# W2 in a ring of row tiles, the second half's products first, and an early turn of the inverse table, in a gated mix of a long convolution and a token MLP

## The chip, the cores and the metric

The kernel runs on one core of a Trainium2 chip. Its engines work side by side, each through its own list of instructions: TensorE (PE) multiplies matrices, VectorE (DVE) and ScalarE (ACT) work on tensors, GpSimd (POOL) here mostly issues the DMAs that add to their target, and SyncE (SP) issues all other DMAs. The metric is device microseconds of one execution.

## The reference

The inputs are q, k, v and x = q of [2048, 640], a long filter per channel, and two weight matrices. The output is `g * a + (1 - g) * b`:

- g is a sigmoid of the row sum of `x * gate_w`, one number per row.
- a = q * (y + kv * ssm_D), where kv = shift(k) * v with four taps per channel, and y is the causal convolution of kv with the filter along the 2048 rows. The reference takes it by FFT of length 4096.
- b is a token MLP: layernorm of x, then `gelu(h^T W1 + b1) W2 + b2`, with W1 [2048, 1536] and W2 [1536, 2048] mixing the rows.

```python
y_f = kv_f * kf_f[None, :, :, :]
y = irfft2(y_f, (1, L))[:, 0, :S, :] + kv * ssm_D
u = gelu(einsum("bsd,sf->bdf", layernorm(x), w1) + b1)
b = einsum("bdf,fs->bds", u, w2) + b2      # transposed back
return g * (q * y) + (1 - g) * b
```

## The kernel before

**The convolution** is a transform written as matmuls. The rows are split by residues, the forward transforms of the filter (W) and of kv (A) are matmuls with a table FTB of sines, and VectorE mixes residues by adds and subtracts (`mixing`, `mixing_acc`). The spectra lie in slots of 2560 columns in the big tiles C[0] to C[3] and SS. V0, V1 are those of the filter and A0, A1 those of kv; each has two groups, 0 and 1, and each group two slots. A slot holds a real part (component 0) and an imaginary one (component 1), so a step on both slots of a group and both parts is 5120 columns wide and a step on one part is 2560.

The two halves of the output need the products `A0 * V0` and `A1 + ...` of complex numbers. Before the products `cross(g)` (L1165) multiplies A0 into V1, in four steps per slot with one DMA that adds a term; V1 then holds a term that is added to A1's product. `product` (L1130) multiplies a group in place: in full it is two multiplies of 5120 columns (into the scratch tiles T0, T1), a subtract and an add. With `late` it is one multiply of 5120 and three steps of 2560, and the second cross term goes by a DMA that adds it to the result. `acc_dma` (L1146) adds V1[g] to A1[g] with two such DMAs. The order is cross 0, cross 1, A0[0], A0[1] (both late), A1[0], A1[1] (both in full, each followed by its `acc_dma`). Then `invmix` (L1177) mixes the two groups of a half in eight steps, and `inverse` (L1196) runs 64 matmuls per half with the table, ScalarE scales by the gate, and VectorE multiplies by q. The first half is Z0 from A0, the second Z1 from A1. Matmuls of `inverse` read the table after it was put in another order: four DMA transposes turn FTB into GTB, and four ScalarE copies ("gil", L1082) write GTB back over FTB. They may run once the forward transforms are done. Before, they come after the inner matmuls, the copies tied to an output tile of the MLP.

**The MLP**: the inner product (m1) is 12 tiles `ft` of 32 matmuls, W1 being the stationary side and X the moving one, W1 coming in three column groups through two buffers `ring[0]` and `ring[1]` of 16 tiles [128, 512] each (`ring[(ft // 4) % 2]`). A GELU on ScalarE makes tile ft of GT. The outer product (m2) is 16 tiles of 24 matmuls, four for each quarter hk of W2's columns. A quarter is [128, 12, 512], loaded in two DMAs of six row tiles. Quarters 0 and 2 lie over ring[1], quarters 1 and 3 over ring[0] (L600), so quarter 1 waits for the last inner tile and quarters 2 and 3 for the outer tiles two quarters before.

**The gate**: `x * gate_w` goes through three small buffers gq that lie on GTB (L589); ScalarE sums them. The inverse's output buffers cgb lie there too.

**The order** of every engine's list is worked out ahead, by a planner (`_Sched`). Each operation has a planned duration, and each engine takes, of the operations ready by the plan, the one with the lowest `prio`, which is its index where none is given. m1 and m2 have priorities above 10^6, so they fill PE wherever the convolution has nothing ready; at most two of the four PSUM slots may hold MLP tiles. An accumulating DMA is planned at 1.2 us to issue, its bytes at 365 GB/s and 8 us to land. `after` means only that the other operation has started in the plan; chain=True orders the SP loads that carry it in this way. On the chip the order of each list is fixed, and each instruction waits by semaphores for what it reads and overwrites.

Of the kernel before, what the change touches and what calls it, by code (L numbers as in the profile page):

```python
# [510 lines left out]
def _build(nc, A_q, A_k, A_v, A_shift_k, A_ssm_k, A_ssm_D, B_x, B_w1, B_b1, B_w2, B_b2, gate_w, out):  # L511
# [10 lines left out]
    with ExitStack() as es:  # L522
# [13 lines left out]
        def alloc(name, shape, dtype, at=None):  # L536
            size = mybir.dt.size(dtype)
            for s_ in shape[1:]:
                size *= s_
            if at is None:  # L540
                off = cur[0]
                cur[0] = (off + size + 63) // 64 * 64
            else:
                off = at
            assert off % 4 == 0 and off + size <= top, f"SBUF overflow {name}: {off}+{size} > {top}"
            h = nc.alloc_sbuf_tensor_at(name, list(shape), dtype, offset=off)
            T.reg_sbuf(h, off)
            return h

        def base_of(h):  # L550
            return T.mem[h.name][1]
# [34 lines left out]
        dif = alloc("dif", [128, 128], I32, at=base_of(SS) + 64 + 1024)  # L586
        dif2 = alloc("dif2", [128, 32], I32, at=base_of(SS) + 64 + 1536)
        KT = [alloc(f"KT{i}", [128, NG, KTW], BF16) for i in range(2)]
        gq = [alloc(f"gq{i}", [128, 2, D], BF16, at=base_of(GTB) + 2560 * i) for i in range(3)]  # L589
        ssm = alloc("ssm", [128, ND, S], BF16, at=base_of(C[3]))  # L590
        wT = alloc("wT", [128, 4, 4, D], BF16, at=base_of(C[2]))
        vkv0 = alloc("vkv0", [128, 2, 4, D], BF16, at=base_of(C[3]))
# [4 lines left out]
        kn = [alloc(f"kn{i}", [128, 4, D], BF16, at=base_of(ring[1]) + 5120 * i) for i in range(2)]  # L597
        kp = [alloc("kp0", [128, NG, 128], BF16, at=base_of(ring[1]) + 10240), alloc("kp1", [128, NG, 128], BF16, at=base_of(GTB))]
        pint = alloc("pint", [128, 4, 2, 2, 256], I32, at=base_of(ring[1]))
        W2 = [alloc(f"W2_{i}", [128, FT, 512], BF16, at=base_of(ring[(i + 1) % 2])) for i in range(2)]  # L600
        O1 = alloc("O1", [128, 4, 4, D], BF16, at=base_of(X))
        tm = [alloc(f"tm{i}", [128, 2, 4, D], BF16, at=E_base + 2 * SL * 2 * i) for i in range(2)]
        q_lo = alloc("q_lo", [128, 2, 4, D], BF16, at=base_of(C[1]) + 2 * SL * 2)
# [111 lines left out]
        def dr(t, off, ap):  # L715
            return bass.AP(tensor=t.tensor, offset=t.offset + off, ap=ap)
# [22 lines left out]
        def w1_load(c, hk):  # L739
            dma(ring[c % 2][:, 4 * hk:4 * hk + 4, :], dr(B_w1, 512 * hk * F + 512 * c, [[4 * F, 128], [F, 4], [1, 512]]), 128 * 4096, chain=True)  # L740
# [239 lines left out]
        for hk in range(4):  # L980
            w1_load(1, hk)

        def v1mix(Wh, Ws, Vh, Vs):
            for i in range(2):
                dma(V(Vh, (Vs + i) * SL, [[1280, 2], [1, 1280]]), V(Wh, (Ws + i) * SL + 1280, [[-1280, 2], [1, 1280]]),
                    128 * 5120, stream="POOL", prio=0, accum=True)
# [58 lines left out]
        for ft in range(FT):  # L1045
            if ft == 4:
                for hk in range(4):
                    w1_load(2, hk)
            vt = _VT("mlp")
            r = ring[(ft // 4) % 2]  # L1050
            col = 128 * (ft % 4)
            for hk in range(4):
                items = []
                for p in range(4):
                    for ci in range(2):
                        items.append((chk(ci), r[:, 4 * hk + p, col:col + 128], X[:, hk, p, 320 * ci:320 * ci + 320],
                                      hk == 0 and p == 0, hk == 3 and p == 3))
                mms(vt, items, prio=10 ** 6 + 4 * ft + hk, name="m1")
            g_ = act(GT[:, ft, :].rearrange("p (a b) -> p a b", a=2), two, ACT.Gelu_apprx_tanh, bias=cc[:, 16 + ft:17 + ft], vt=vt, prio=0, name="gelu")
            if ft == 0:  # L1060
                act(gq[2][:, 0, :], gwb[:, :], ACT.Copy, acc=gws[:, :], name="gws").after.add(g_)
            if ft in (1, 3, 5, 7):
                hk = ft // 2
                for a in range(2):
                    gb = gq[(2 * hk + a) % 3]
                    tt("DVE", gb[:, :, :], X[:, hk, 2 * a:2 * a + 2, :], V(gwb, 0, [[0, 2], [1, D]]), ALU.mult)
                    for b in range(2):
                        t = 4 * hk + 2 * a + b
                        act(gb[:, b, :], gb[:, b, :], ACT.Copy, acc=gacc[:, t:t + 1], name="gsum")
# [7 lines left out]
        tt("DVE", c2[:, :].rearrange("p (a b) -> p a b", a=4), omg[:, :].rearrange("p (a b) -> p a b", a=4), b2f, ALU.mult, mode=1, prio=0)  # L1077

        gils = []
        for p in range(4):  # L1080
            dma(GTB[:, p, :, :, :, :].rearrange("q a b c d -> q (a b c) d"), FTB[:, p, :, :, :, :].rearrange("q a b c d -> q (a b c) d"), 128 * 2048, rate=200.0, transpose=True, prio=10 ** 5)
            gil = act(V(FTB, 1024 * p, [[1, 2], [256, 4], [2, 128]]), V(GTB, 1024 * p, [[512, 2], [128, 4], [1, 128]]), ACT.Copy, prio=10 ** 5, name="gil")  # L1082
            gils.append(gil)

        HORD = (0, 1, 2, 3)
        lastvt = []
        for n_, hk in enumerate(HORD):
            W2h = W2[n_ % 2]
            for a in range(2):
                w2last = dma(W2h[:, 6 * a:6 * a + 6, :], dr(B_w2, a * 6 * 128 * S + 512 * hk, [[S, 128], [128 * S, 6], [1, 512]]), 128 * 6144)  # L1090
            for p in range(4):
                vt = _VT("mlp")
                t = 4 * hk + p
                last_ = n_ == 3 and p == 3
                order = [(ft, ci) for ci in range(2) for ft in range(FT)] if last_ else [(ft, ci) for ft in range(FT) for ci in range(2)]
                na = 2 if last_ else 3
                for a in range(na):
                    items = []
                    for ft, ci in order[a * (24 // na):(a + 1) * (24 // na)]:
                        items.append((chk(ci), V(W2h, ft * 512 + p, [[4, 128]]), GT[:, ft, 320 * ci:320 * ci + 320], ft == 0, ft == FT - 1))  # L1100
                    mms(vt, items, prio=2 * 10 ** 6 + 4 * (4 * n_ + p) + a, name="m2")
                    if last_:
                        vt.keep = True
                        lastvt.append(vt)
                if not last_:
                    o_ = act(O1[:, hk, p, :].rearrange("p (a b) -> p a b", a=2), two, ACT.Identity, bias=c2[:, t:t + 1], scale=omg[:, t:t + 1], vt=vt, name="o1")
                    if n_ == 1 and p == 2:
                        for g in gils:
                            g.after.add(o_)

        A0 = {0: (C[2], 2), 1: (C[1], 0)}
        A1 = {0: (C[3], 2), 1: (C[3], 0)}
# [14 lines left out]

        npr = [0]

        def product(dst, a, v, late=False):  # L1130
            tt("DVE", P2(T0), P2(a), P2(v), ALU.mult)
            if late:
                n_ = npr[0] % 2
                npr[0] += 1
                tt("DVE", V(q_hi, n_ * SL, [[1280, 2], [1, 1280]]), H(a, 1), H(v, 0), ALU.mult)
                tt("DVE", H(dst, 1), H(a, 0), H(v, 1), ALU.mult)
                tt("DVE", H(dst, 0), H(T0, 0), H(T0, 1), ALU.subtract)
                dma(H(dst, 1), V(q_hi, n_ * SL, [[1280, 2], [1, 1280]]), 128 * 5120, stream="POOL", prio=0, accum=True)
# [38 lines left out]
        def invmix(Ya, Yb, sc, z0, z2):  # L1177
            def sl(h, s):
                return V(h, s * SL, [[1, SL]])

            def pr(h, s, rev=False):
                return V(h, s * SL + (1280 if rev else 0), [[-1280 if rev else 1280, 2], [1, 1280]])
            (ha, sa), (hb, sb), (hs, ss) = Ya, Yb, sc
            tt("DVE", sl(hs, ss), sl(ha, sa), sl(ha, sa + 1), ALU.add)
            tt("DVE", sl(hs, ss + 1), sl(hb, sb), sl(hb, sb + 1), ALU.add)
            tt("DVE", sl(ha, sa), sl(ha, sa), sl(ha, sa + 1), ALU.subtract)
            tt("DVE", sl(hb, sb), sl(hb, sb), sl(hb, sb + 1), ALU.subtract)
            tt("DVE", sl(ha, sa + 1), sl(hs, ss), sl(hs, ss + 1), ALU.add)
# [54 lines left out]
        Z0 = invmix(A0[0], A0[1], C3a, None, None)  # L1243
# [40 lines left out]
```

## Time and profile before

| | |
|---|---|
| median of 4 runs | 188.74 us (187.06 to 191.86) |
| profiled execution | 191.69 us |
| its span | 189.6 us |
| PE busy | 179.2 us (94%), 1389 matmuls |
| VectorE busy | 169.6 us (89%) |
| ScalarE busy | 117.3 us (62%) |
| GpSimd busy | 49.9 us (26%) |
| granted clock of PE | 0.991 |
| DMA | 42.86 MB, 226 GB/s |

The span runs from the first to the last instruction of the profiled execution. A slice of the page is a fortieth of the span, 4.74 us. In the waits, the first number is the sum in us, then how often, then the longest. PE's 384 inner and 384 outer matmuls and the 352 of the transforms of 320 columns follow each other at 0.136 us (24 of an outer tile in 3.26 us), though a single one is shown with 299 ns, as they overlap.

### The profile page before, as it was taken

To read this page: it belongs to the slowest core of one execution; us is meant where nothing else is said; L and a number is where in the kernel's file an instruction comes from. 1 tells how busy PE (TensorE), PEld (TensorE's weight loads), DVE (VectorE), ACT (ScalarE), POOL (GpSimd) and SP (SyncE) were. 2 spreads that over 40 slices of the span, in tenths; PEclk is the share of its full clock that TensorE was granted. 3 is DMA by queue.
4 is the path that set the end of the run, shared out by engine and by line. 5 is a ranking of instruction groups with operands and counts; after the bars stand their busy time and mean duration, and the time that the engine had idled before them with its cause. 6 is when DMAs were issued, how large, how long until landed. Compare 5 with 4: busy or idle time off the path is not lost.

```text
span 189.6 us, 3344 instructions
## 1 busy us (share of the span) xinstructions
PE 179.2 (94%) x1389; PEld 130.1 (69%) x1390; DVE 169.6 (89%) x200; ACT 117.3 (62%) x176; POOL 49.9 (26%) x41
## 2 busy tenths in 40 slices
PE   7999899989999998999999999999999999939994
PEld 3565486658778675766777778868888866826683
DVE  8699895999699999999889999999999998498553
ACT  5599987799999999169972111312493157314730
POOL 4059604599000252002212110102050504320000
PEclk9999999999999999999999999999999999997999
DMA  5999999899992399994899999999989999994332
GB/s 158 381 409 371 388 213 240 340 420 212 165 348 60 111 165 193 266 238 91 140 207 274 112 134 124 177 298 322 288 230 262 251 263 299 201 232 107 138 107 104
DMA packets 38206, 42.86 MB, mean 226 GB/s; under 512 B 15787, under 2 KB 31280, under 8 KB 38192
## 3 DMA queue, kind: packets, MB, share of 16 engines
q1 hardware_dynamic: 33232, 32.16, 58.5%
q0 software_dynamic: 4928, 10.49, 33.6%
q8 instruction: 11, 0.18, 0.4%
q14 instruction: 3, 0.02, 0.0%
q10 hardware_dynamic: 32, 0.01, 0.0%
HBM read 25.87 MB, written 2.62 MB: 150 GB/s over the span
## 4 chain that ended last, share of the span: by engine, by line
PE 38%; DVE 26%; ACT 19%; DMA 11%; issue 4%; POOL 0%; SPq 0%; DVEq 0%
PE pp L293 38%; DVE C L624 14%; ACT C L668 10%; DMA C<-C 8%; DVE tm L624 7%; ACT gq L668 5%; DVE q_hi L624 3%; DMA ssm<-in_A_ssm_k_dram 3%; ACT GT L668 2%; ACT FTB L668 1%; DVE SS L624 1%; ACT L668 1%; ACT wT L668 1%; POOL C L262 0%; DVE O L680 0%
## 5 line engine op out<-in xcount | busy, mean ns | idle before, releaser
L293 PE MATMUL pp<-X,ring 128*128 128x320 bf16 x384 | 54.9, 299 | 0.7 <-ACT GT L668 0.7
L293 PE MATMUL pp<-GT,W 128*128 128x320 bf16 x384 | 53.0, 299 | 0.3 <-DMA W<-in_B_w_dram 0.3
L624 DVE TENSOR_TENSOR C<-C 128x2560 bf16<-128x2560 bf16 (+2 forms) x34 | 51.7, 1564 | 0.1
L293 PEld LDWEIGHTS pp<-GT,W 128*128 128x128 bf16 x384 | 43.3, 114 | 9.6 <-DMA W<-in_B_w_dram 0.9
L293 PEld LDWEIGHTS pp<-X,ring 128*128 128x128 bf16 x384 | 37.3, 98 | 15.3 <-issue 1.0
L668 ACT ACTIVATE C<-pp 128x640 bf16<-128x640 f32 x64 | 40.2, 722 | 4.2 <-PE pp L293 4.1
L668 ACT ACTIVATE O<-pp,c,omg 128x640 bf16<-128x640 f32 x15 | 13.2, 881 | 30.8 <-PE pp L293 30.8
L262 POOL DMA_DIRECT2D C<-C x8 | 9.9, 1359 | 49.9 <-DVE C L624 46.4
L293 PE MATMUL pp<-wT,FTB 128*128 128x320 bf16 x128 | 19.9, 301 | 2.0 <-ACT C L668 1.2
L668 ACT ACTIVATE GT<-pp,cc 128x640 bf16<-128x640 f32 x12 | 9.6, 799 | 15.4 <-PE pp L293 15.4
L668 ACT ACTIVATE cgb<-pp,gg 128x640 bf16<-128x640 f32 x16 | 12.7, 793 | 10.3 <-PE pp L293 10.3
L293 PEld LDWEIGHTS pp<-wT,FTB 128*128 128x128 bf16 x128 | 11.0, 98 | 10.1 <-ACT C L668 4.8
L293 PE MATMUL pp<-C,FTB 128*128 128x320 bf16 x96 | 15.0, 321 | 2.9 <-DVE C L624 2.9
L913 DVE BATCH_NORM_STATS2 stats<-X 128x6 f32<-128x320 bf16 x32 | 13.7, 464 | 1.7 <-DMA X<-in_A_q_dram 1.7
L293 PEld LDWEIGHTS pp<-C,FTB 128*128 128x128 bf16 x96 | 9.5, 105 | 8.2 <-issue 3.2
L262 POOL DMA_DIRECT2D C<-q_hi x6 | 5.9, 977 | 32.4 <-DVE C L624 28.8
L624 DVE TENSOR_TENSOR tm<-C,C 128x2560 bf16<-128x2560 bf16 (+1 forms) x7 | 14.3, 2058 | 0.0
L624 DVE TENSOR_TENSOR SS<-C 128x2560 bf16<-128x2560 bf16 x8 | 11.6, 1487 | 2.6 <-DMA C<-C 2.5
L1016 POOL COPY KT<-KT 128x20 bf16<-128x20 bf16 x1 | 12.4, 12379 | 3.1 <-DMA KT<-kp 3.1
L624 DVE TENSOR_TENSOR C<-tm 128x2560 bf16<-128x2560 bf16 (+1 forms) x10 | 12.0, 1221 | 0.1
L668 ACT ACTIVATE gq<-gq 128x640 bf16<-128x640 bf16 x16 | 11.8, 743 | 0.0
L668 ACT ACTIVATE wT<-pp 128x1024 bf16<-128x1024 f32 x10 | 9.6, 1032 | 1.6 <-PE pp L293 1.6
(72 smaller groups left out, 197.8 us busy)
## 6 DMA issues: line engine op xcount, KB each, us to landing
ring<-in_B_w_dram SPq DMA_DIRECT2D x12, 512.0 KB, 10.3
W<-in_B_w_dram SPq DMA_DIRECT2D x8, 768.0 KB, 9.6
C<-C POOLq DMA_DIRECT2D x8, 640.0 KB, 10.7
X<-in_A_q_dram SPq DMA_DIRECT2D x4, 640.0 KB, 9.0
kn<-in_A_k_dram SPq DMA_DIRECT2D x4, 640.0 KB, 8.4
out_dram<-O SPq DMA_DIRECT2D x7, 320.0 KB, 3.4
ssm<-in_A_ssm_k_dram SPq DMA_DIRECT2D x3, 512.0 KB, 6.4
vkv<-in_A_v_dram SPq DMA_DIRECT2D x2, 640.0 KB, 5.4
```

Of the source, the lines that this page charges most:

```text
L262: ins = engobj.dma_start(out_ap, in_ap, accum_op=ALU.add, max_dma_last_dim=2560)
L293: ins = self.nc.tensor.matmul(ps_ap, lhsT=lhsT, rhs=rhs, start=start, stop=stop, skip_group_check=True)
L624: o_ = SC.add(eng, d, lambda s: T.op(eng, lambda e: e.tensor_tensor(o, a, b, op), rd, [o]), rd, [o], prio=prio, name="tt")
L668: return T.op("ACT", lambda e: e.activation(o, src, func, **kw), rr + [src], ww)
L913: ops.append(SC.add("DVE", 0.38, (lambda o, i: lambda s: T.op("DVE", lambda e: e.bn_stats(o, i), [i], [o]))(o, i), [i], [o]))
L1016: SC.add("POOL", 0.3, lambda s: T.op("POOL", lambda e: e.tensor_copy(KT[1][:, :, 15:16], KT[0][:, :, 143:144]), [KT[0][:, :, 143:144]], [K ...
```

## The change

Five things change.

1. **W2** is one tile of 32 slots over both rings. A quarter is loaded in three DMAs of four row tiles, into the slots of the list W2S: quarter 0 to 20, 24, 28, quarter 1 to 16, 0, 4, quarter 2 to 8, 12, 20, quarter 3 to 24, 28, 16.
2. **The products** come in the order A1[1], A1[0], A0[1], A0[0], each chained behind the start of the one before. A1's are no longer in full: their second cross term goes by DMA into V1, which `acc_dma` then adds to A1. A0[1]'s goes by DMA from V0[1]'s place; A0[0]'s product is in full.
3. **`acc_dma`** for A1[1] and A1[0] follows the first two products, and in `invmix` the two steps on the first group come ahead of those on the second.
4. **The table's transposes** are chained behind the second group of W1 loads, and the ScalarE copies come at ft = 9, after the GELU of ft = 8 has started.
5. **gq** has two buffers, on the second half of q_hi (which holds the taps table KF early and the scratch of `cross` later).

```diff
-        gq = [alloc(f"gq{i}", [128, 2, D], BF16, at=base_of(GTB) + 2560 * i) for i in range(3)]
+        gq = [alloc(f"gq{i}", [128, 2, D], BF16, at=base_of(Drow) + 5120 + 2560 * i) for i in range(2)]
...
-        W2 = [alloc(f"W2_{i}", [128, FT, 512], BF16, at=base_of(ring[(i + 1) % 2])) for i in range(2)]
+        W2 = alloc("W2", [128, 32, 512], BF16, at=base_of(ring[0]))
...
             w1_load(1, hk)
 
+        gtbs = []
+        for p in range(4):
+            gtbs.append(dma(GTB[:, p, :, :, :, :].rearrange("q a b c d -> q (a b c) d"), FTB[:, p, :, :, :, :].rearrange("q a b c d -> q (a b c) d"), 128 * 2048, rate=200.0, transpose=True, chain=True))
...
+            if ft == 9:
+                for p in range(4):
+                    gil = act(V(FTB, 1024 * p, [[1, 2], [256, 4], [2, 128]]), V(GTB, 1024 * p, [[512, 2], [128, 4], [1, 128]]), ACT.Copy, prio=10 ** 5, name="gil")
+                    gil.after.add(g_)
...
-                act(gq[2][:, 0, :], gwb[:, :], ACT.Copy, acc=gws[:, :], name="gws").after.add(g_)
+                act(gq[1][:, 0, :], gwb[:, :], ACT.Copy, acc=gws[:, :], name="gws").after.add(g_)
...
-                    gb = gq[(2 * hk + a) % 3]
+                    gb = gq[a]
...
-        for p in range(4):
-            dma(GTB[:, p, :, :, :, :].rearrange("q a b c d -> q (a b c) d"), FTB[:, p, :, :, :, :].rearrange("q a b c d -> q (a b c) d"), 128 * 2048, rate=200.0, transpose=True, prio=10 ** 5)
-            gil = act(V(FTB, 1024 * p, [[1, 2], [256, 4], [2, 128]]), V(GTB, 1024 * p, [[512, 2], [128, 4], [1, 128]]), ACT.Copy, prio=10 ** 5, name="gil")
-            gils.append(gil)
-
         HORD = (0, 1, 2, 3)
+        W2S = ((20, 24, 28), (16, 0, 4), (8, 12, 20), (24, 28, 16))
...
-            for a in range(2):
-                w2last = dma(W2h[:, 6 * a:6 * a + 6, :], dr(B_w2, a * 6 * 128 * S + 512 * hk, [[S, 128], [128 * S, 6], [1, 512]]), 128 * 6144)
+            for a in range(3):
+                w2last = dma(W2[:, W2S[n_][a]:W2S[n_][a] + 4, :], dr(B_w2, a * 4 * 128 * S + 512 * hk, [[S, 128], [128 * S, 4], [1, 512]]), 128 * 4096)
...
-                    if n_ == 1 and p == 2:
-                        for g in gils:
-                            g.after.add(o_)
...
-        def product(dst, a, v, late=False):
-            tt("DVE", P2(T0), P2(a), P2(v), ALU.mult)
-            if late:
-                n_ = npr[0] % 2
-                npr[0] += 1
-                tt("DVE", V(q_hi, n_ * SL, [[1280, 2], [1, 1280]]), H(a, 1), H(v, 0), ALU.mult)
+        def product(dst, a, v, late=None, into=None):
+            if into is not None:
+                tt("DVE", late, H(a, 1), H(v, 0), ALU.mult)
+                dma(H(into, 1), late, 128 * 5120, stream="POOL", prio=0, accum=True)
+                tt("DVE", P2(T0), P2(a), P2(v), ALU.mult)
                 tt("DVE", H(dst, 1), H(a, 0), H(v, 1), ALU.mult)
                 tt("DVE", H(dst, 0), H(T0, 0), H(T0, 1), ALU.subtract)
-                dma(H(dst, 1), V(q_hi, n_ * SL, [[1280, 2], [1, 1280]]), 128 * 5120, stream="POOL", prio=0, accum=True)
                 return
+            tt("DVE", P2(T0), P2(a), P2(v), ALU.mult)
+            if late is not None:
+                tt("DVE", late, H(a, 1), H(v, 0), ALU.mult)
+                tt("DVE", H(dst, 1), H(a, 0), H(v, 1), ALU.mult)
+                tt("DVE", H(dst, 0), H(T0, 0), H(T0, 1), ALU.subtract)
+                dma(H(dst, 1), late, 128 * 5120, stream="POOL", prio=0, accum=True)
+                return
...
             tt("DVE", sl(hs, ss), sl(ha, sa), sl(ha, sa + 1), ALU.add)
+            tt("DVE", sl(ha, sa), sl(ha, sa), sl(ha, sa + 1), ALU.subtract)
             tt("DVE", sl(hs, ss + 1), sl(hb, sb), sl(hb, sb + 1), ALU.add)
-            tt("DVE", sl(ha, sa), sl(ha, sa), sl(ha, sa + 1), ALU.subtract)
...
-        for g in range(2):
-            product(A0[g], A0[g], V0[g], True)
+        def tmp_of(h, s_):
+            return V(h, s_ * SL, [[1280, 2], [1, 1280]])
+
+        def chained(f, *a):
+            n0 = len(SC.ops)
+            f(*a)
+            new = [o for o in SC.ops[n0:] if o.eng == "DVE"]
+            for o in new:
+                o.after.update(lastp[-1:])
+            lastp.append(new[-1])
+
+        lastp = []
+        chained(product, A1[1], A1[1], V0[1], tmp_of(q_hi, 0), V1[1])
+        chained(product, A1[0], A1[0], V0[0], tmp_of(q_hi, 1), V1[0])
         for kt in range(2):
             dma(q_hi[:, kt, :, :], dr(A_q, 512 * kt * D, [[4 * D, 128], [1, 4 * D]]), 128 * 5120)
-        for g in range(2):
-            product(A1[g], A1[g], V0[g])
-            acc_dma(A1[g], V1[g])
+        acc_dma(A1[1], V1[1])
+        acc_dma(A1[0], V1[0])
+        chained(product, A0[1], A0[1], V0[1], H(V0[1], 0))
+        chained(product, A0[0], A0[0], V0[0])
```

More of the change, by code (lines that the diff above doesn't have):

```diff
@@ L599, in _build @@
         pint = alloc("pint", [128, 4, 2, 2, 256], I32, at=base_of(ring[1]))
-        W2 = [alloc(f"W2_{i}", [128, FT, 512], BF16, at=base_of(ring[(i + 1) % 2])) for i in range(2)]
+        W2 = alloc("W2", [128, 32, 512], BF16, at=base_of(ring[0]))
+        assert base_of(ring[1]) == base_of(ring[0]) + 16384
         O1 = alloc("O1", [128, 4, 4, D], BF16, at=base_of(X))
@@ L1079, in _build @@
         gils = []
-        for p in range(4):
-            dma(GTB[:, p, :, :, :, :].rearrange("q a b c d -> q (a b c) d"), FTB[:, p, :, :, :, :].rearrange("q a b c d -> q (a b c) d"), 128 * 2048, rate=200.0, transpose=True, prio=10 ** 5)
-            gil = act(V(FTB, 1024 * p, [[1, 2], [256, 4], [2, 128]]), V(GTB, 1024 * p, [[512, 2], [128, 4], [1, 128]]), ACT.Copy, prio=10 ** 5, name="gil")
-            gils.append(gil)
         HORD = (0, 1, 2, 3)
+        W2S = ((20, 24, 28), (16, 0, 4), (8, 12, 20), (24, 28, 16))
         lastvt = []
         for n_, hk in enumerate(HORD):
-            W2h = W2[n_ % 2]
-            for a in range(2):
-                w2last = dma(W2h[:, 6 * a:6 * a + 6, :], dr(B_w2, a * 6 * 128 * S + 512 * hk, [[S, 128], [128 * S, 6], [1, 512]]), 128 * 6144)
+            for a in range(3):
+                w2last = dma(W2[:, W2S[n_][a]:W2S[n_][a] + 4, :], dr(B_w2, a * 4 * 128 * S + 512 * hk, [[S, 128], [128 * S, 4], [1, 512]]), 128 * 4096)
             for p in range(4):
@@ L1099, in _build @@
                     for ft, ci in order[a * (24 // na):(a + 1) * (24 // na)]:
-                        items.append((chk(ci), V(W2h, ft * 512 + p, [[4, 128]]), GT[:, ft, 320 * ci:320 * ci + 320], ft == 0, ft == FT - 1))
+                        items.append((chk(ci), V(W2, (W2S[n_][ft // 4] + ft % 4) * 512 + p, [[4, 128]]), GT[:, ft, 320 * ci:320 * ci + 320], ft == 0, ft == FT - 1))
                     mms(vt, items, prio=2 * 10 ** 6 + 4 * (4 * n_ + p) + a, name="m2")
```

## The prediction

> **What bounds the kernel now.** I read the page's slices first, then the waits of PE, then the timeline of PE, then the chain that ended last, then single landings. The slices, 4.74 us each:
>
> ```profile
> PE   7999899989999998999999999999999999939994
> DVE  8699895999699999999889999999999998498553
> PEclk9999999999999999999999999999999999997999
> DMA  5999999899992399994899999999989999994332
> ```
>
> From slice 15 on PE is full but for one hole at slice 35 and the slice at the end, and right behind the hole the clock is down. So the time is the sum of the matmuls plus what PE stands idle. The waits of PE say how much that is:
>
> ```profile
> PE pp L293 <- DVE C L624: 2.9, 1, 2.9
> PE pp L293 <- ACT GT L668: 1.5, 2, 0.8
> PE pp L293 <- DVE cst L684: 1.2, 1, 1.2
> ...
> PE pp L293 <- DMA W<-in_B_w_dram: 0.3, 1, 0.3
> ```
>
> One wait of 2.9 us stands out. The timeline of PE (start, length) places it between the two halves of the inverse transform:
>
> ```profile
> 111.81 14.96 PE L293 MATMUL pp<-GT,W 128*128 128x320 bf16 x108
> 127.09 25.73 PE L293 MATMUL pp<-GT,W 128*128 128x320 bf16 x188 [0.32 <-DMA W<-in_B_w_dram]
> 152.72 8.87 PE L293 MATMUL pp<-C,FTB 128*128 128x320 bf16 x64
> 161.42 5.60 PE L293 MATMUL pp<-GT,W 128*128 128x320 bf16 x40
> 169.91 6.12 PE L293 MATMUL pp<-C,FTB 128*128 128x320 bf16 x32 [2.90 <-DVE C L624]
> 175.87 4.51 PE L293 MATMUL pp<-SS,FTB 128*128 128x320 bf16 x32
> 180.24 6.71 PE L293 MATMUL pp<-GT,W 128*128 128x320 bf16 x48
> ```
>
> The first 32 matmuls after the hole take 6.12 us, the next 32 only 4.51: 1.6 us more, with a granted clock of 0.68 from 170 to 175 us. Two W2 tiles (48 matmuls) are left for the end although PE had nothing to do at 167: the instruction order is fixed, so filler isn't pulled forward. The chain says who was late:
>
> ```profile
> 147.94 0.73 POOL C L262
> 148.66 15.97 DMA C<-C
> 164.64 0.03 issue
> ...
> 164.73 1.49 DVE SS L624
> 166.23 0.73 DVE q_hi L624
> 166.96 2.82 DVE C L624 x2
> ...
> 169.91 17.05 PE pp L293 x112
> ```
>
> The last accumulating DMA of A1[1] (the sum A1 += V1, L1146) starts at 148.7, because product A1[1] is the last of the four, lands 16.0 us later, and the second inverse mix waits 2.5 us on VectorE for it. What is to be had: 2.90 (hole) + 1.61 (clock) + 0.32 (W2) = 4.8 us. More there is not: the rest of PE's idle time is the start, a wait for ACT at 72, and 2.6 us after the last matmul, none of which the change removes.
>
> **The change, part by part.** *Order of the products.* VectorE is dense from 113.56, when the crosses are done, to 152. A multiply of 5120 takes 2.82 us, of 2560 1.49. Before: six of the first and ten of the second, 31.8 us. After: A1[1] and A1[0] with their cross term sent through a DMA (1+3 each), A0[1] likewise (1+3), A0[0] in full (2+2): 5 x 2.82 + 11 x 1.49 = 30.5. The chained order leaves nothing to put between dependent steps; the rows show 1.53 between dependent starts against 1.40 between independent ones, some eight times, so I take back 0.8 and credit 0.5 us. Products end near 144.9, and the first two steps of the first inverse mix, put ahead because they read A0[0] alone, end near 147.7.
>
> *The A1 sums.* The late term of A1[1] is ready at 115, of A1[0] near 125 (its scratch is that of the last cross, whose DMA, issued at 113.2, landed 9.4 us later). The A1[1] sums can go at about 126.5, the A1[0] sums at about 135. Even with 16 us each they are in by 152 to 153; the second inverse mix asks for them from 155 on. The 2.5 us wait on VectorE, and with it the hole on PE, should go: -2.9, and the clock with it, -1.6.
>
> *What is late next: A0[1].* This is a new wait. A0[1] += its late term (one more DMA of 640 KB) is ready at 113.6 + 7.3 + 7.5 + 5.7 = 134.1, and the mix needs it at 147.7: 13.6 us. If it is later, VectorE waits, behind it the rest of both mixes, and PE, whose order is fixed, waits at the first inverse matmul. The rows for a 640 KB accumulation:
>
> ```profile
> C<-C POOLq DMA_DIRECT2D x1, 640.0 KB, 7.2
> ```
> ```profile
> C<-q_hi POOLq DMA_DIRECT2D x1, 640.0 KB, 9.5
> ```
> ```profile
> C<-C POOLq DMA_DIRECT2D x1, 640.0 KB, 12.7
> ```
>
> These were issued at 91.4 on a quiet queue, at 129.7 among loads, and at 138.3 as the first of a pair; the worst is the 16.0 of the chain. The Trainium skill (DMA: Bandwidth & Descriptors, Anatomy of one DMA — SWDGE path) gives 2.0 us plus bytes over 436 GB/s for such a DMA: 3.5 us for 640 KB. By that it lands at 137.6 and there is nothing to fear; by the rows between 141 and 150, so no wait to 2.4 us. I go by the rows. In the queue it stands behind the A1[1] pair issued near 126.5; the four sums of before landed at 151.0, 154.1, 159.7 and 164.6, some 3 to 5.5 us apart, so after a pair done near 142 it lands at about 147. I take 0.7 us of PE time, ends 0 and 2.4.
>
> The same skill (TensorE: Matmul & The Clock Gate, Part 1) tells to avoid PE-idle gaps over about 3.4 us, which would leave a 2.9 us gap uncooled. The trace differs: 2.9 us of idle was followed by the half clock. By the rule the hole cost 2.9, by the row 4.5; and a new wait of 2 to 3 us is then also to be charged with up to 1.6 more.
>
> *W2.* Eight loads of 768 KB become twelve of 512 KB: the same bytes, four more issues of 0.4 us on SP, which is idle then. Hidden: the first four go at about 92 to 95, the next four as the last inner tile frees its slots (109 to 112), against 116.8 to 125.7 before; PE asks for the second quarter at 125 and the third at 138. A 512 KB load landed in 4 to 16 us. -0.3, and if the cover were gone, at worst the 0.3 stays.
>
> *The table.* Its four transposes held SP from 94.5 to 116.7 and kept the second quarter of W2 behind them. Now they stand behind the second inner load, issued by 52 us. They hold SP perhaps 22 us again; behind them are only the third inner loads (62.4 to 71.7 now), which are needed near 95. DMA is at 0.72 busy from 48 to 72 us. The accumulations of 65 to 71 landed by 85 and are asked for at 88 and 100. 0; at worst 1 us. The four copies that put the table in place (1.35 us each) move from 136 to the gaps of 3.3 to 3.5 us between gelus after 99: 0.
>
> *Smaller things.* The gate's buffers are two and lie on the taps and on the scratch of the second cross. The gate-weight sum (0.78 + 0.24 us, ACT at 42.5) must now wait for the taps' last matmul at 59.7 and falls into ACT's dense stretch, which ends with PE's wait of 0.7 at 72. ACT has the same work before 72 either way: 0, ends -0.5 and +1. The gate's products may wait a little more on ACT (0.75 once now): 0 on PE.
>
> **Sum.** The profiled execution took 191.7 us: the span of 189.6 and 2.1 around it. -4.8 + 0.7 = -4.1 gives 187.6. It was 2.95 us longer than the median of 188.74, so the median run presumably has a smaller hole. With the wait but not the half clock in it, the median loses 3.2 and pays 0.7: 186.2. If all of 4.8 is in it and nothing new comes: 183.9. If all of the 2.95 was stall, 1.9 is left to gain: 187.5. I take 186.2.
>
> **Rivals.** (1) The hole moves: A0[1] lands near 150, PE waits 2 us ahead of the first inverse half and runs 1 us worth of slow clock. 188.7 - 3.2 + 3 = 188.5. For it: 4.6 MB of accumulation between 115 and 150, at some 5 us for 0.64 MB, is 35 us of a queue that has 35. Against it: W2's last loads now come earlier, and in the old window there were 768 KB loads beside the sums. (2) Slower: POOL's order is fixed too, by planned times, and the plan has the A1[0] sums and the A0[1] term ready within a few us of each other. If the sums come first, A0[1] goes at 137.5 behind four, lands near 155, and VectorE stands 7 us; PE, its filler planned for less, loses 5 and 1.6 of clock: 188.7 - 3.2 + 6.6 = 192.1, at milder planning error 190. It decides from a landing near 151 on. Against it: the late term of A1[0] is held to 125 by the cross's scratch, so its landing (134.5) comes after 134.1, though barely. (3) The table's transposes collide with the accumulations before the crosses and VectorE starts the products late: 188 to 190. The slack of 3 to 15 us speaks against it.
>
> **Chances.** Forecast (183.5 to 187.3): 0.52. Rival 1: 0.2. Rival 2: 0.22. Rival 3: 0.06. A change of 1% (1.9 us) is about what a measurement of this kernel can tell from none, as its runs spread over 187.1 to 191.9. Faster by over 1% is below 186.85: most of the forecast, 0.49. Within 1%: 0.26. Slower: 0.25. The range of 183.6 to 190.8 leaves out the top of rival 2 and little else.
>
> **What would show it.** Right: no gap on PE at 167, the clock full to the end, no DVE wait for a DMA in the second mix, W2 waits gone, the table's transposes at 52 to 72, A1's sums issued near 126 and 135. Wrong: a PE wait just ahead of the first inverse matmul near 152, with VectorE waiting for DMA on the first mix; the A0[1] accumulation landing after 148; VectorE reaching the products later than 113.6; a new PE gap at 72.

## The result

The changed kernel takes 186.66 us in the median of 44 executions (185.6 to 189.26), the kernel before 189.09 us in that of 73 (186.12 to 196.35). The ratio is 0.9949, with a 95% interval of 0.9929 to 0.9968: a gain of about 0.5%. The executions of one kernel differ by several microseconds, those of before by more. The ratio counts only the executions within 1.5% of the shortest of their kernel, 38 of the 44 but 33 of the 73, while the medians count all and are 1.3% apart, so before's long executions, like the profiled one of 191.69 us, hardly enter it. The forecast of 186.2 us stood for a gain of 1.35%. That it lay near the median is luck: the part that it named as the cause brings no gain at all, as the experiments show.

The profiled execution of the changed kernel has a span of 184.3 us, against 189.6. Its slices, 4.6 us each:

```profile
PE   7879899989999999999999999999999999899994
DVE  8779895999999999999989999999999696999773
DMA  5999999999999999993999778959999998199363
```

The hole of PE at slice 35 is gone; there is a small dip at slice 34. No slice has a clock under full. PE's timeline (start, length) from the first outer matmul:

```profile
110.70 41.46 PE L293 MATMUL pp<-GT,W 128*128 128x320 bf16 x304
152.00 4.51 PE L293 MATMUL pp<-C,FTB 128*128 128x320 bf16 x32
156.34 1.25 PE L293 MATMUL pp<-GT,W 128*128 128x320 bf16 x8
157.43 0.43 PE L293 MATMUL pp<-C,FTB 128*128 128x320 bf16 x2
158.66 4.25 PE L293 MATMUL pp<-C,FTB 128*128 128x320 bf16 x30 [0.80 <-DVE C L625]
...
176.03 5.60 PE L293 MATMUL pp<-GT,W 128*128 128x320 bf16 x40
```

The wait has moved from between the halves into the first half, and it is 0.80 us long. The first outer matmul starts at 110.70 us, in the profile of before at 111.81. Only 0.24 us of that is an effect of the change. From the matmul for which PE waits near 39 us (0.78 us, for a GELU) to the first outer matmul it is 72.08 to 72.10 us in the eight usual profiles without the table's part and 71.84 to 71.87 us in the nine with it, where PE's next wait, near 72 us, is 0.35 us instead of 0.71. The rest differs from one execution to the next: the first loads of the filter land at different times (PE begins on the second of them between 5.7 and 6.6 us), and in four profiles, that of before among them, PE takes 1.07 us instead of 0.71 for each eight matmuls on the filter until about 12 us. The start in the 17 usual profiles of this study wanders from 109.9 to 112.0. So I compare the stretch from the first outer matmul to the end of the last one, 512 matmuls in every kernel here: 176.03 + 5.60 - 110.70 = 70.9 us, before 180.24 + 6.71 - 111.81 = 75.1. VectorE and the chain say what PE waited for:

```profile
145.73 7.10 DVE L625 TENSOR_TENSOR C<-C 128x2560 bf16<-128x2560 bf16 x5 [1.84 <-DMA C<-SS]
154.31 1.49 DVE L625 TENSOR_TENSOR SS<-C 128x2560 bf16<-128x2560 bf16 x1 [1.48 <-DMA C<-C]
155.72 2.89 DVE L625 TENSOR_TENSOR C<-C,C 128x2560 bf16<-128x2560 bf16 x2
```
```profile
123.78 10.92 DMA C<-q_hi
...
134.99 0.73 POOL C L262
135.72 18.50 DMA C<-C
...
154.31 0.54 DVE SS L625
...
155.72 2.90 DVE C L625 x2
158.62 0.05 issue
158.66 22.97 PE pp L293 x166
```

VectorE waits twice. The first wait, 1.84 us, is the new one, for A0[1]'s late term. The second is for the last A1[0] sum. It was issued at 135.7 and took 18.5 us, longer than the 16.0 of before. The step that waits for it belongs to the second half's mix, but in VectorE's list it stands ahead of the last two steps of the first half's mix, and PE needs those for the residues 1 and 3.

### The profile page after: what moved, and what is told of

Read it like the earlier page. It is cut to its first block, busy times and chain, and to the rows that moved or that the text cites. A ratio compares the mean times of both kernels' runs of the same rounds, so it can differ in the third digit from the quotient of the medians.

```text
span 184.3 us, 3350 instructions
## 1 busy us (share of the span) xinstructions
PE 175.4 (95%) x1389; PEld 128.3 (70%) x1390; DVE 168.4 (91%) x200; ACT 117.1 (64%) x176; POOL 39.1 (21%) x42
## 4 chain that ended last, share of the span: by engine, by line
PE 48%; DMA 19%; DVE 14%; ACT 13%; issue 4%; POOL 0%; SPq 0%; DVEq 0%
PE pp L293 48%; DMA C<-C 10%; DVE C L625 8%; ACT C L669 6%; DMA C<-q_hi 6%; DMA ssm<-in_A_ssm_k_dram 3%; DVE q_hi L625 2%; DVE tm L625 2%; ACT wT L669 2%; ACT gq L669 2%; ACT GT L669 1%; ACT FTB L669 1%; ACT L669 1%; POOL C L262 0%; DVE O L681 0%
## 5 line engine op out<-in xcount | busy, mean ns | idle before, releaser
L293 PEld LDWEIGHTS pp<-X,ring 128*128 128x128 bf16 x384 | 37.1, 98 | 15.1 <-issue 0.7
L262 POOL DMA_DIRECT2D C<-C x8 | 10.4, 1484 | 47.1 <-DVE C L625 46.1
L293 PE MATMUL pp<-C,FTB 128*128 128x320 bf16 x96 | 13.7, 299 | 0.8 <-DVE C L625 0.8
L625 DVE TENSOR_TENSOR tm<-C,C 128x2560 bf16<-128x2560 bf16 (+1 forms) x7 | 14.3, 2057 | 0.0
L625 DVE TENSOR_TENSOR SS<-C 128x2560 bf16<-128x2560 bf16 x8 | 11.6, 1487 | 1.5 <-DMA C<-C 1.5
L293 PEld LDWEIGHTS pp<-C,FTB 128*128 128x128 bf16 x96 | 8.9, 98 | 5.2 <-DVE C L625 1.1
L625 DVE TENSOR_TENSOR C<-tm 128x2560 bf16<-128x2560 bf16 (+1 forms) x9 | 10.6, 1192 | 0.1
L262 POOL DMA_DIRECT2D O<-q_hi x4 | 4.8, 1324 | 25.0 <-DVE q_hi L625 25.0
```

Of the source, the lines that this page charges most:

```text
L262: ins = engobj.dma_start(out_ap, in_ap, accum_op=ALU.add, max_dma_last_dim=2560)
L293: ins = self.nc.tensor.matmul(ps_ap, lhsT=lhsT, rhs=rhs, start=start, stop=stop, skip_group_check=True)
L625: o_ = SC.add(eng, d, lambda s: T.op(eng, lambda e: e.tensor_tensor(o, a, b, op), rd, [o]), rd, [o], prio=prio, name="tt")
```

## The experiments

A column of the table below is worked out in the same way for each kernel: the stretch is the end of the last outer matmul less the start of the first. Times are medians; the ratio is against before on the same chip, with its interval.

| kernel | us | ratio | stretch, us | PE waits in it, us |
|---|---|---|---|---|
| before, first profile | 189.09 | 1 | 75.1 | 0.32 + 2.90, then half clock |
| b_again | 188.91 | 0.997 [0.9925, 1.0014] | 71.9 | 1.88 |
| b_cut | 186.77 | 0.9876 [0.9832, 0.9920] | 69.9 | none |
| b_plan5 | 187.44 | 0.9937 [0.9897, 0.9977] | 69.8 | none |
| order_only | 193.90 | 1.0057 [1.0005, 1.0108] | 74.2 | 2.63, then half clock |
| table_only | 188.06 | 0.9988 [0.9957, 1.0019] | 74.2 | 2.50, then half clock |
| w2_only | 186.10 | 0.9903 [0.9870, 0.9935] | no usual profile | |
| w2_again | 186.79 | 0.9921 [0.9882, 0.9960] | 71.4 | 1.35 |
| order_w2 | 188.74 | 1.0009 [0.9975, 1.0043] | 72.6 | 1.25 + 0.88 |
| w2_table | 185.80 | 0.9875 [0.9816, 0.9934] | 69.9 | none |
| w2_table_again | 184.78 | 0.9841 [0.9778, 0.9905] | 69.9 | none |
| w2_plan | 186.41 | 0.9950 [0.9906, 0.9994] | 69.8 | none |
| changed kernel | 186.66 | 0.9949 [0.9929, 0.9968] | 70.9 | 0.80 |
| after_again | 185.96 | 0.9892 [0.9831, 0.9953] | 70.7 | 0.57 |
| a_cut01 | 184.60 | 0.9836 [0.9785, 0.9887] | 69.9 | none |
| a_plan | 184.90 | 0.9859 [0.9798, 0.9920] | 69.9 | none |
| a_plan_again | 185.41 | 0.9857 [0.9792, 0.9923] | 69.9 | none |
| a_full01 | 185.57 | 0.9872 [0.9809, 0.9935] | 69.9 | none |

69.9 us is the floor: 512 matmuls at 0.1365 us. Whatever a kernel here has above it is, to about 0.5 us, PE's waiting and the half clock after a long wait.

**How large is the hole of before?** First the kernel before again, without an edit.

> The kernel before, unchanged, profiled again. My theory: the hole on PE before the second inverse half belongs to every execution, and its length is set by how long the last A1[1] sum takes to land (16.0 us in the first profile). Then a new profile with a landing of 11 to 13 us shows a hole of 0 to 1 us, a full clock, and a time near 187; with 16 us again it shows 2.9 us and 190 or more. Rival: the hole is the same 2.9 us in any execution and the 4 us between the first profile and the usual time lie elsewhere (start, first loads, clock).

PE's timeline of this second profile of before, and its chain:

```profile
160.06 5.60 PE L293 MATMUL pp<-GT,W 128*128 128x320 bf16 x40
167.53 4.54 PE L293 MATMUL pp<-C,FTB 128*128 128x320 bf16 x32 [1.88 <-DVE C L624]
```
```profile
147.95 14.31 DMA C<-C
```

The sum took 14.3 us instead of 16.0, the hole is 1.88 us instead of 2.90, and the 32 matmuls after it take 4.54 us, at full clock. PE's wait for W2 is absent. So this execution, of 187.87 us, has 71.9 - 69.9 = 2.0 us to gain, not the 4.8 of the first profile. The theory was right in kind, though a landing of 14.3 fell between the two cases that I had named.

Then the hole taken away, with every order kept: the A1[1] sums move 64 of 1280 columns, so part of a term is missing from the second half.

```diff
+                n_ = 64 if dst == A1[1] else 1280
-                o = V(hd, (sd + i) * SL, [[1280, 2], [1, 1280]])
-                i_ = V(hs, (ss + i) * SL, [[1280, 2], [1, 1280]])
+                o = V(hd, (sd + i) * SL, [[1280, 2], [1, n_]])
+                i_ = V(hs, (ss + i) * SL, [[1280, 2], [1, n_]])
```

> Before, with the two sums A1[1] += V1[1] moving 64 of 1280 columns each, planned as if whole, so that every engine's order stays; the rest of the sum is left out, so the second half of the output lacks part of a term. My theory: the hole and the half clock go, and what is left is the gain that the whole change can have in the usual execution: 1 to 3 us below before, 184.5 to 186.5. Rival (the usual execution has no hole): within 0.5 us of before.

It gained 1.24%, 2.3 us in the medians, and reached the floor:

```profile
166.08 4.54 PE L293 MATMUL pp<-C,FTB 128*128 128x320 bf16 x32
```

The landing of that sum is the whole hole.

And the hole filled instead: the planner is told that the A1 sums land 5 us later, so PE's list has 36 more outer matmuls ahead of the second half.

```diff
-                    op.end = dma_free + 2.0 + (6.0 if e == "POOL" else 0.0)
+                    op.end = dma_free + 2.0 + (6.0 if e == "POOL" else 0.0) + (5.0 if op.name in ('sum',) else 0.0)
...
-                dma(o, i_, 128 * 5120, stream="POOL", prio=0, accum=True)
+                dma(o, i_, 128 * 5120, stream="POOL", prio=0, accum=True).name = "sum"
```

> Before, with the planner told that the four sums A1 += V1 land 5 us later than it thought, and nothing else. On PE the same instructions, but 76 outer matmuls instead of 40 ahead of the second inverse half and 12 instead of 48 at the end. My theory: the hole is a planning error, since PE had 48 matmuls of filler left; the filler closes it without any change of products or loads, and the time is that of the changed kernel or within 0.7 us of it, 186 to 187, with VectorE's wait for the sum unchanged at 1 to 3 us. Rival (the sum itself must land earlier, or the shorter filler at the end lays bare the last steps of VectorE): no gain, or 1 us slower.

It gained 0.63%: VectorE still waits 1.2 us for the sum, and PE waits for nothing. But the chain of this kernel ends otherwise than that of before (PE's filler between the halves first, then the chain):

```profile
159.19 10.49 PE L293 MATMUL pp<-GT,W 128*128 128x320 bf16 x76
```
```profile
149.92 28.50 PE pp L293 x209
178.42 0.02 issue
178.45 0.80 ACT cgb L668
179.25 0.02 issue
179.27 0.84 DVE cgb L624
```

The chain leaves PE at 178.4 us, with the transform's last matmul: 12 outer matmuls are too few to cover what ScalarE and VectorE still do with it. PE ends at 180.0 and the span at 184.1, 4.1 us later, where before has 2.7. So part of the 2 us is given back at the end. By the ratios, one edit of the plan, without any other order of products, gains as much as the whole change did.

**Which part of the change does it?** Here the edit is a part of the diff above. The order of the products alone (points 2 and 3 of the change):

> Before, with the new order of products, the A1 sums after the first two and the new order in the inverse mix; W2, table and gate buffers as before. My theory: this alone brings what the change brings, 0.5 to 1.2 us below before in the median, with A1's sums issued near 127 and 137 us, no hole before the second half, and a VectorE wait of 0 to 3 us in the first mix. Rival (the gain is in the loads and the table): within 0.3 us of before, because the table's transposes and the 768 KB loads slow the A0[1] term and the sums, and a hole of 1 to 3 us opens before the first half.

It lost 0.6% by the ratio and 2.6% in the medians of all, 193.90 against 189.07 us; its executions spread from 188.7 to 207.6 us. The profiled one, of 190.60 us, is among the shorter; what the longer ones lose was not profiled. Its PE timeline and its chain:

```profile
153.56 2.33 PE L293 MATMUL pp<-GT,W 128*128 128x320 bf16 x8 [2.63 <-DMA W<-in_B_w_dram]
155.68 5.03 PE L293 MATMUL pp<-C,FTB 128*128 128x320 bf16 x32
```
```profile
136.82 0.02 issue
136.83 0.02 SPq L196
136.85 0.03 issue
136.88 16.64 DMA W<-in_B_w_dram
153.52 0.05 issue
153.56 32.27 PE pp L293 x224
```

It is neither the theory nor the rival. VectorE did wait 3.2 us in the first mix, but PE was held first by W2: the last quarter may only be loaded when the outer tiles of the second quarter are done (SP's wait ends at 136.83), and just then, with the new order, the A1 sums and A0[1]'s term are in flight. A load of 768 KB took 16.6 us.

The ring alone (point 1), in two runs, and the table with the gate's buffers alone (points 4 and 5):

> Before, with W2 in the ring of 32 slots and in thirds, nothing else. My theory: only the 0.3 us wait of PE for W2 goes, and the sums of A1 have less beside them at 138 to 155 us, so the last one may land 1 to 3 us earlier; 0.2 to 1.0 us below before. Rival (W2 has no part in it): within 0.3 us.

> Before with W2 in the ring and in thirds alone, profiled again (its first profile caught an execution with PE at a sixth of its speed). It was 1.0% below before, more than the 0.3 us of PE's W2 wait. My theory: the ring takes 768 KB loads away from beside the A1 sums, so the last A1[1] sum lands in 10 to 13 us instead of 14 to 16, VectorE waits 0 to 1 us for it, and the hole on PE is at most 0.7 us. Rival: the sum lands as late as before (14 to 16 us, hole 2 to 3 us), and the gain comes from PE's order, which has 8 filler matmuls inside the first half.

> Before, with the table turned behind the second group of inner loads, its copies at ft = 9, and the gate's two buffers on q_hi. My theory: 0 in the sum, so within 0.4 us of before; the transposes take about 10 us of SP instead of 22. Rival (it has a price, the gate-weight sum in ACT's dense stretch): up to 1 us slower with a longer PE wait near 72 us.

The ring alone gained 0.97% and 0.79%. In the second run's profile:

```profile
147.65 13.05 DMA C<-C
```
```profile
166.71 4.54 PE L293 MATMUL pp<-C,FTB 128*128 128x320 bf16 x32 [1.35 <-DVE C L625]
```

The last A1[1] sum lands in 13.05 us, and the hole is 1.35 us. That is less than in either profile of before, but a little more than the theory had it. One profile against one gives 0.5 us; over all executions the ring gains more. The rival, PE's order, falls away: with its eight filler matmuls inside the first half PE still has 400 matmuls ahead of the second half, as before. But VectorE now does one more step of 0.74 us between the sum and PE, which takes back part of the 1.26 us that the sum lands earlier than in b_again.

That the ring lets the A1 sums land sooner is seen in more than this pair. The slowest of the four sums took 16.0, 14.4, 15.1 and 15.7 us in the profiles of the old order without the ring (before, b_again, b_plan5, table_only), and 13.1, 11.6, 11.6 and 12.8 us in those with it (w2_again, w2_plan, and the two of ring and table below). Just ahead of the sums b_again issues two loads of 768 KB, w2_again one of 512 KB:

```profile
136.32 1.41 SPq L267 DMA_DIRECT2D W<-in_B_w_dram  x2
```
```profile
134.95 0.37 SPq L267 DMA_DIRECT2D W<-in_B_w_dram  x1
```

Whether it is the smaller loads or their earlier place was not tried apart.

The table alone is level with before, with a hole of 2.50 us. It does shift one thing: the A1[1] sums are issued 145.72 - 110.24 = 35.48 us after the first outer matmul, where both profiles of before have 36.13. VectorE reaches them 0.65 us earlier.

Two parts at a time:

> The new order of products and W2's ring together; table and gate buffers as before. The order alone was 0.6% slower, because the second load of W2's last quarter landed 16.6 us after it could start and PE stood 2.6 us for it. My theory: with the ring that wait is gone and the two together are level with the whole change, 0.3 to 0.9% below before, so the table has no part. Rival (the table's transposes at 94 to 113 us hold W2's and the sums' queue back here too): 0 to 0.3% slower than before.

> W2's ring and the early table, with the products in the old order. My theory: the order of the products brings nothing once the ring is there; this is 0.7 to 1.3% below before, at or below the whole change. Rival (the order is worth its 2 us of hole): 0.3% below before or less.

The order with the ring is level with before, and so 0.9% behind the ring alone on the same chip: W2's wait is gone, and in its place are two waits for VectorE in the first half and a landing of 20.8 us.

```profile
154.35 4.51 PE L293 MATMUL pp<-C,FTB 128*128 128x320 bf16 x32 [1.25 <-DVE C L625]
...
161.25 4.25 PE L293 MATMUL pp<-C,FTB 128*128 128x320 bf16 x30 [0.88 <-DVE C L625]
```
```profile
135.96 20.84 DMA C<-C
```

The ring with the table, in the old order of products, gained 1.25% by its ratio, where the changed kernel gained 0.51%. Both once more, beside each other on one chip:

> The changed kernel, unchanged, beside the next three on one chip. My theory: it stays 0.3 to 0.8% below before, its profile again shows VectorE waits of 1 to 4 us in all for A0[1]'s term and for the A1 sums, a landing of 16 to 20 us for the last A1 sum, and 0 to 1.5 us of PE wait in the first inverse half. Rival (the first profile of it was a chance): landings of 10 to 13 us and no wait.

> W2's ring and the early table with the products in the old order, once more, beside the changed kernel. My theory: the new order of products costs what the ring and the table bring; this is 0.9 to 1.4% below before and 0.4 to 1.0% below the changed kernel, with the last A1 sum landing in 10 to 13 us. Rival (the six runs of it were a lucky sample): level with the changed kernel within 0.3%.

The changed kernel shows its waits and its late landing again (18.3 us for the last sum, 0.57 us of PE wait), and gains 1.1% in this set, more than the 0.3 to 0.8% expected. Six executions each: 185.36 to 187.26 for the changed kernel and 184.53 to 185.93 for ring and table, where four of the six lie below the fastest of the changed kernel. The medians differ by 1.2 us, the stretches by 0.8 (and by 1.0 between the first profiles of each). PE of w2_table_again:

```profile
150.32 4.52 PE L293 MATMUL pp<-C,FTB 128*128 128x320 bf16 x32
154.68 1.25 PE L293 MATMUL pp<-GT,W 128*128 128x320 bf16 x8
155.77 4.51 PE L293 MATMUL pp<-C,FTB 128*128 128x320 bf16 x32
160.11 4.51 PE L293 MATMUL pp<-GT,W 128*128 128x320 bf16 x32
164.46 4.57 PE L293 MATMUL pp<-C,FTB 128*128 128x320 bf16 x32
```

No wait. In the profiles of these two runs no 640 KB accumulation from 110 us on took longer than 11.6 and 12.8 us.

**What of the new order costs?** Two cuts and a plan on the changed kernel. First A0[1]'s late term moving 64 of 1280 columns:

```diff
-                dma(H(dst, 1), late, 128 * 5120, stream="POOL", prio=0, accum=True)
+                (hd, sd), (hs, ss) = dst, V0[1]
+                dma(V(hd, sd * SL + 1280, [[SL, 2], [1, 64]]), V(hs, ss * SL, [[SL, 2], [1, 64]]), 128 * 5120, stream="POOL", prio=0, accum=True)
```

> The changed kernel, with the DMA that adds A0[1]'s late term moving 64 of 1280 columns, planned as whole; the rest of that term is left out. My theory: VectorE's wait of 1.8 us in the first mix goes, the A1 sums behind it in the queue land 2 to 4 us earlier, so that the wait of 1.5 us for them goes too, and PE loses its 0.8 us wait: 0.5 to 1.0 us below the changed kernel. Rival (A0[1]'s new DMA costs nothing on PE): within 0.3 us of it.

Then A0[1]'s product in full on VectorE, without that DMA:

```diff
-        chained(product, A0[1], A0[1], V0[1], H(V0[1], 0))
+        chained(product, A0[1], A0[1], V0[1])
```

> The changed kernel with A0[1]'s product in full on VectorE (two multiplies of 5120 columns, no late term): one accumulation of 640 KB fewer, 1.3 us more on VectorE, same result. My theory: the new DMA is what costs (it waits behind the A1 sums and holds them); without it VectorE's waits go, and it is 0.3 to 0.8% below the changed kernel. Rival (VectorE is the limit there, so 1.3 us more work costs 1 us): 0.2 to 0.5% above it.

Then the changed kernel with the plan told of later landings, 6 us for the A1 sums and 2 us for A0[1]'s late term:

```diff
-                    op.end = dma_free + 2.0 + (6.0 if e == "POOL" else 0.0)
+                    op.end = dma_free + 2.0 + (6.0 if e == "POOL" else 0.0) + {'sum': 6.0, 'late': 2.0}.get(op.name, 0.0)
```

> The changed kernel, with the planner told that the A1 sums land 6 us later and the A0 late terms 2 us later than it thought. PE gets 8 outer matmuls more before the first half, 8 more within it and 16 fewer between. My theory: the 0.8 us wait of PE at 158 us is gone and the spread of the runs shrinks; 0.3 to 0.9 us below the changed kernel, about 1% below before. Rival: less filler between the halves opens a new hole before the second half, and it is level with the changed kernel or slower.

> The changed kernel with the planner told of later landings (6 us for the A1 sums, 2 us for the A0 term), once more. My theory: what the new order costs is the unplanned PE wait in the first half; with filler put there it is 0.5 to 1.0% below the changed kernel and level with the ring and the table alone. Rival (the crowded queue costs elsewhere too): within 0.3% of the changed kernel.

All three reach the floor. In a_cut01, where PE's order is that of the changed kernel, VectorE's wait in the first mix is gone, the one for the sums is 1.1 us, and PE's is gone:

```profile
151.25 1.49 DVE L625 TENSOR_TENSOR SS<-C 128x2560 bf16<-128x2560 bf16 x1 [1.14 <-DMA C<-C]
```
```profile
156.62 4.58 PE L293 MATMUL pp<-C,FTB 128*128 128x320 bf16 x32
```

In a_full01 VectorE waits for no accumulation at all, in spite of 1.3 us more work, though its plan also puts 16 more outer matmuls ahead of the first half. In a_plan VectorE still waits 0.7 us for A0[1]'s term, but PE has filler there. So the price of the new order is the added DMA, through a fixed list of PE that counted on it sooner. On one chip with after_again, a_plan_again is 0.55 us and a_full01 0.39 us below it in the median; that is less than expected of either, and with six executions each it is shown by the waits rather than by the times. The profiled executions of a_plan and a_plan_again, 186.53 and 184.72 us, have the same stretch and differ in its start alone, 112.0 and 110.1 us.

The last one puts the ring and the plan together, with the old order:

> W2's ring, old order of products, and the planner told that the A1 sums land 5 us later than it thought, which puts 76 outer matmuls instead of 40 ahead of the second inverse half. My theory: both remedies together leave no hole however late the sum is, 1.2 to 1.7% below before and the smallest spread. Rival (the ring alone has closed the hole already): the same as the ring alone, 1.0%, or up to 0.3% more for the bare end.

It gained 0.5%, no more than the ring alone, whose interval overlaps with its own. PE waits for nothing and the stretch is 1.6 us shorter than in w2_again, but the 12 matmuls at the end leave the same bare end as in b_plan5 (PE ends at 180.4, the span at 184.4), 1.3 us longer than in w2_again. The theory was wrong here: once the hole is small, filler taken from the end costs there nearly all that it saves.

## Why the prediction was right or wrong

**The bound** was read rightly: the time is the sum of the matmuls plus PE's waits. Every kernel above has its stretch at 69.9 us plus its waits and the half clock, to about 0.5 us.

**The size of the hole** was wrong. The sum of -4.8 + 0.7 = -4.1 us against the profiled execution came out at 75.1 - 70.9 = -4.2, but that execution was a long one. "The median run presumably has a smaller hole", with 3.2 us to lose, was a guess. It was 2.0 us in the second profile of before (1.88 of hole, no half clock, no W2 wait), and 2.3 us in the medians of b_cut. With 0.8 for the new wait, 1.2 us or 0.6% is left, and 0.5% was measured. The case of 187.5 us, named in the sum for "1.9 left to gain", was the right one, and it was not taken.

**The order of the products** was credited with nearly the whole gain, the hole and the clock behind it; that step failed. Moving A1's sums to 126 and 135 us did happen as worked out (they were issued from 124.5 and 135.0 on), and the wait before the second half went. But the last of them took 18.5 us to land: seven accumulations of 640 KB are now issued within 22 us (113.7 to 135.7), before it was six within 26 us (122.3 to 148.7). With one of the seven left out, in a_full01, the last two land after 14.8 us in the mean instead of 17.1. Alone the order costs 0.6% or more; with the ring it takes the ring's gain away; on top of ring and table it costs 0.8 to 1.2 us. What gains in its place is the ring with the table in the old order, 1.25% and 1.59%.

**When the second mix asks for the sums**: "from 155 on" was wrong. Its first step stands in VectorE's list before the last steps of the first mix, was due at 152.8, and so the late sum held up the first half.

**The new wait for A0[1]**, rival 1, was placed and nearly sized. The term was ready near 132.7 (134.1 predicted, with an earlier start), landed after 13.0 us by the trace, VectorE waited 1.84 us (0 to 2.4 predicted). PE waited 0.80 us (0.7), but behind both of VectorE's waits, the second of which the prediction did not have; so the good size is in part luck. The 3.5 us that the prediction worked out by the Trainium skill (DMA: Bandwidth & Descriptors, Anatomy of one DMA — SWDGE path) is far from the 13.0 here; the decision for the rows was right.

**W2** was costed at -0.3 us, its cover at nothing more. That was the largest miss. The ring alone gains 0.8 to 1.0%, about 1.5 to 1.9 us; the slowest A1 sum lands in 11.6 to 13.1 us instead of 14.4 to 16.0; and without the ring the new order stands 2.6 us for the last quarter. The one pair of profiles shows 0.5 us of that gain, and the rest stays open. In the costing I looked at when PE asks for W2 and not at what W2's loads do to the accumulations beside them.

**The table** at 0: right alone within the noise, with 0.24 us gained ahead of the stretch. With the ring it closes the rest of the hole (71.4 us in one profile to 69.9 in two); 0.65 us of that is VectorE reaching the sums earlier, the rest is a landing that was shorter. The table is not needed for such a landing: the slowest sum of w2_plan, which lacks the table, took 11.6 us too. The transposes took SP 10 us instead of 22, not the 22 that I had allowed:

```profile
L260 SPq DMA_TRANSPOSE GTB<-FTB x4: 1311/2330/3994, 53.2 to 62.0; - x4
```

Rival 2 (the sums ahead of A0[1]'s term on GpSimd) did not happen: the term went at 132.7, the A1[0] sums at 135.0. Rival 3 did not happen either; VectorE reached the products at 111.9.

## What to carry to other kernels

One profile of a kernel whose executions differ is one draw: profile it twice, and cut the suspected transfer to a sliver with the order kept, before counting what its removal is worth. Where a list is fixed by a plan, the plan's landing times are part of the kernel; filler put where transfers really land did as much as a new order of the work, and cost time again where too little was left to cover the end. And loads that are made smaller and moved earlier are worth what they do to the transfers that they no longer stand beside, which can be more than the wait for the loads themselves.

## What the runs showed of the hardware

The half clock followed the longer waits only. PE idle for 1.88 us (b_again) was followed by 32 matmuls in 4.54 us, with a granted clock of 1.00; idle for 2.50 us (table_only) by 32 in 6.18 us, with 0.80 from 170 to 175 us; and for 2.90 us (before) by 32 in 6.12. After 2.63 us in order_only eight matmuls took 2.33 us instead of 1.25, with a clock of 0.55 from 153 to 156 us. Where between 1.88 and 2.50 us it turns, and whether the length alone decides, four waits do not show. The limit of about 3.4 us that the prediction quoted from the Trainium skill (TensorE: Matmul & The Clock Gate, Part 1) is too high for these runs.

The first profile of w2_only caught an execution of 1023 us. PE waited for no DMA, and the longest wait for one, of VectorE, was 11.3 us; PE itself was slow, with a mean granted clock shown as 1.00. The row for its first 296 outer matmuls, and the same row in w2_again:

```profile
595.21 245.00 PE L293 MATMUL pp<-GT,W 128*128 128x320 bf16 x296
```
```profile
110.80 40.37 PE L293 MATMUL pp<-GT,W 128*128 128x320 bf16 x296
```

That is a sixth of the speed. It was seen once in all executions here, and its cause stays open. The slower start of four profiles, 1.07 us instead of 0.71 for eight matmuls, does not show in the granted clock either: it is 1.00 from 5 to 10 us in those too.
